# All steps of a planned kernel in a new order: both scaled copies of px ahead of both VectorE mixes

## The chip, the cores and the metric

The kernel runs on one core of a Trainium2 chip. The metric is the device time of one execution in microseconds (us). Engines are called TensorE (PE; its weight loads PEld), VectorE (DVE), ScalarE (ACT), GpSimd (POOL) and SyncE (SP), the last of which only issues DMAs here.

## The reference

Two layers follow one another, for a batch of 4 with 12288 positions of 128 channels each. The first is attention over 768 pooled keys, which are also the values:

```
kv_flat = kv.reshape(B, H//4, 4, W//4, 4, C).mean(axis=(2, 4)).reshape(B, -1, C) @ w_sr
s = (q @ kv_flat.transpose(0, 2, 1)) / sqrt(C)
a = exp(s - s.max(-1)); a /= a.sum(-1) + 1e-9
x = a @ kv_flat
```

The second mixes each position with the one before it and gates a squared ReLU:

```
xk = mu_k * x + (1 - mu_k) * x_prev
xr = mu_r * x + (1 - mu_r) * x_prev
v = maximum(xk @ w_k, 0) ** 2 @ w_v        # w_k 128 x 1024, w_v 1024 x 128
out = v / (1 + exp(-(xr @ w_r)))
```

## The kernel before, in words

The positions of all batches are cut into 96 tiles of 512 (24 to a batch). Each tile is a list of named steps, `plan_tile` (line 506); a step is a few instructions of one engine. For tile i, with s from 0 to 3 (quarters of 128 positions), f from 0 to 3 (quarters of the 1024 inner channels) and j from 0 to 5 (blocks of 128 keys):

- `qf` loads q (SP), `qh` and `ql` split it into two parts (ScalarE, GpSimd). `S`s is six products (three splits times two pieces of the keys) into a PSUM buffer S, `nm`s its negated row maximum (VectorE), `ex`s the exponential with its row sum (ScalarE), `rc`1 and `rc`3 the reciprocals of two sums (VectorE, two small instructions). `f1`s and `f2`s make the two half-precision parts of the scaled row, tile pp (ScalarE, VectorE); `tt`s transposes it by DMA into pT (SP).
- `AV`j is three products each, 18 in all, that sum up in one PSUM bank, px. From px ScalarE makes two scaled copies, `xek` and `xer`, one column to the right, and VectorE two mixes, `xk` and `xr`, which add px, scaled again, to the copy. `xck` and `xcr` (GpSimd) bring the last column of the tile before. `xkh`, `xrh` (VectorE) and `xkl`, `xrl` (GpSimd) split the mixes into two half-precision parts.
- `ha`f and `hb`f are four and two products into a PSUM buffer ph, `r`f the ReLU (ScalarE, tile rr), `k2`f the square (VectorE, but ScalarE for f = 2), `kh`f and `kl`f its two parts (`kl`0 to `kl`2 are GpSimd's; `kl`3 and `kh`2 VectorE's). `va`f and `vb`f are four and two products into the PSUM bank pv.
- `z` is three products into pz, `th` and `E` two functions of it (ScalarE), `T1`, `E1`, `g` and `o` (VectorE) the gate and its product with pv; `so` stores o (SP).

PSUM holds three buffers of two banks, which S and ph take in turn (eight in a tile), one bank for px and pz (and for the small products of the keys), and one for pv. Where two engines read one PSUM buffer, the second waits until the first is done, whichever the order written; so `xek` behind `xr` waits for it, and `z` waits until all four readers of px are done.

The first batch's keys and the split weights come from steps that occur once: `L_` loads into six buffers in turn, `pa` and `pb` products with w_sr, `ab` sums on VectorE, and steps beginning with w for the weights. The next batch's keys are made beside the tiles (`later_keys`, line 382, and `batch_prep`, line 424): twelve sums `br` on VectorE, one a tile, and then, in about four tiles, `pk`, `pt` (TensorE), `ks`, `v1` (ScalarE), `am`, `ex`, `ksv`, `dg`, `v2`, `xt`, `sv`, `uz`, `ksh` (VectorE), `ksl` (GpSimd). `pk` and `pt` take the bank of px, so that a `z` or a first `AV` behind them waits until `ks` or `v1` and `v2` have read it; `v20` reads the first `pt`, `v21` the second.

The order is written out in tables of due times. `plan.add(places[name] + base, name, fn, ...)` puts each step of each tile on one list, sorted by due time, and the instructions are issued in that order; each engine keeps it:

```python
if i < len(EARLY):
    places, base = EARLY[i], 0.0
elif i >= NTILES - len(LATE):
    places, base = LATE[i - (NTILES - len(LATE))], i * PERIOD
else:
    places, base = WHEN, i * PERIOD
```

`WHEN` holds for tiles 6 to 91, shifted by PERIOD = 19.3 from tile to tile, `EARLY` and `LATE` for the first six and last four tiles, `PREP` for a next batch's keys (from 18 periods after the batch's first tile) and `ONCE` for the rest. A due time only sorts: an instruction starts when its engine has come to it and its waits are over. All tiles in the steady state thus show the same order, in which steps of five or six tiles interleave.

Every instruction goes through one helper, so the profile puts all of them on line 37 and tells them apart by tile names.

Of the kernel before, what the change touches and what calls it, by code (L numbers as in the profile page):

```python
# [71 lines left out]
def tile_kernel(ctx, tc, qT, kv0, kvw, w_sr, mu_k, mu_r, w_k, w_v, w_r, outT):  # L72
# [730 lines left out]
    for i, (b, t) in enumerate(seq):  # L803
# [39 lines left out]
    "ksl": 94.358,  # L843
# [38 lines left out]
        "xek": 93.799, "xer": 93.801, "xr": 94.755, "xk": 94.904, "xkh": 96.037, "xrh": 96.843,  # L882
# [7 lines left out]
    },  # L890
    {
# [15 lines left out]
    },  # L907
    {
# [195 lines left out]
```

## Time and profile before

| what | value |
|---|---|
| median of 3 runs | 1945.48 us (1943.72 to 1945.65) |
| the profiled execution | 1945.21 us, span of its instructions 1943.4 us |
| mean granted clock of TensorE | 0.992 |
| busy: PE, DVE, ACT, POOL | 1883.7, 1801.5, 1693.8, 1096.1 us (97%, 93%, 87%, 56% of the span) |
| matmuls, other instructions of DVE, ACT, POOL | 8883; 2582, 2432, 784 |
| first S product of tile 0 | 26.63 us |

Busy is the time that an engine had an instruction under way, also one that is held up inside. Matmuls overlap one another, so a mean duration of 380 ns for a product does not mean that two take 760 ns. Some matmul records are missing from the trace, mainly of `vb`.

### The profile page before, as it was taken

Reading aid. Unit: us, or ns where it says so; the run is one execution under the profiler, and the core shown is the slowest. Engines: PE = TensorE matmul, PEld = TensorE weight load, DVE = VectorE, ACT = ScalarE, POOL = GpSimd, SP = SyncE. Lnnn points to the kernel's source line nnn. Section 1 sums busy time; section 2 is a strip of 40 time slices with the busy share of each in tenths; the row PEclk is TensorE's granted clock in tenths of the full one; section 3 lists DMA queues with packets and bytes.
Section 4 is the critical chain, followed back from the end, with each engine's and each line's share of the span. In section 5 each row is a group of like instructions: output and inputs, shape, how many; then the busy total and the mean of one; then the engine's idle time right before and its main releaser. Section 6 shows DMA issues by size and latency. Waiting matters only on the chain. (4 is left out here: it accounts for less than half of the span.)

```text
span 1943.4 us, 26996 instructions
## 1 busy us (share of the span) xinstructions
PE 1883.7 (97%) x8883; PEld 1042.4 (54%) x9022; DVE 1801.5 (93%) x2582; ACT 1693.8 (87%) x2432; POOL 1096.1 (56%) x784
## 2 busy tenths in 40 slices
PE   6699999999999999999999999999999999999999
PEld 4345555555555555555555555555555555555554
DVE  6899999999999999999999999999999999999998
ACT  3688989888989898988999898987899999999997
POOL 0365565565656565546565656565565555556565
PEclk9799999999999999999999999999999999999999
DMA  6546575545565656445465656554555554645452
GB/s 210 116 106 152 116 156 111 102 103 107 110 131 130 147 125 147 104 101 111 99 124 118 154 125 147 125 114 87 109 109 114 103 121 97 128 98 122 88 120 60
DMA packets 640524, 230.59 MB, mean 119 GB/s; under 512 B 606336, under 2 KB 608640, under 8 KB 640384
## 3 DMA queue, kind: packets, MB, share of 16 engines
q1 hardware_dynamic: 640384, 228.85, 54.5%
q8 instruction: 72, 1.18, 0.3%
q14 instruction: 68, 0.56, 0.1%
HBM read 52.63 MB, written 25.17 MB: 40 GB/s over the span
## 5 line engine op out<-in xcount | busy, mean ns | idle before, releaser
L37 POOL TENSOR_TENSOR kl<-kk,kh 128x1024 bf16<-128x1024 f32 x288 | 673.0, 2338 | 633.5 <-DVE kk L37 508.8
L37 DVE TENSOR_REDUCE nm<-S 128x1 f32<-128x768 f32 x384 | 364.8, 951 | 82.4 <-PE S L37 80.3
L37 PE MATMUL px<-pT,v 128*128 128x512 f16 x1728 | 420.7, 380 | 2.5 <-DVE xk L37 2.0
L37 ACT ACTIVATE rr<-ph 128x1024 f32<-128x1024 f32 x384 | 392.5, 1023 | 9.4 <-PE ph L37 8.1
L37 PE MATMUL S<-ksh,ql 128*128 128x512 f32 (+1 forms) x768 | 314.2, 409 | 13.9 <-ACT pe L37 4.8
L37 ACT ACTIVATE kh<-rr 128x1024 f16<-128x1024 f32 x288 | 306.1, 1063 | 1.7 <-PE pv L37 0.7
L37 PE MATMUL ph<-xkh,wkl 128*128 128x512 f16 x768 | 292.1, 380 | 15.9 <-ACT rr L37 15.4
L37 PE MATMUL pv<-kh,wvl 128*128 128x512 f16 x768 | 292.1, 380 | 2.8
L37 DVE SCALAR_TENSOR_TENSOR pp<-pe,rc,pp 128x768 f16<-128x768 f32 x288 | 291.6, 1037 | 1.0 <-ACT pp L37 0.5
L37 PE MATMUL ph<-xkh,wkh 128*128 128x512 f16 x768 | 291.9, 380 | 0.0
L37 PE MATMUL pv<-kh,wvh 128*128 128x512 f16 x768 | 291.1, 379 | 0.0
L37 PEld LDWEIGHTS <-v 128*128 128x128 f16 x1728 | 169.2, 98 | 207.1 <-issue 4.8
L37 ACT ACTIVATE pp<-pe,rc 128x768 f16<-128x768 f32 x288 | 259.3, 930 | 7.8 <-DVE rc L37 6.7
L37 ACT ACTIVATE pe<-S,nm 128x768 f32<-128x768 f32 x288 | 260.8, 906 | 5.1 <-DVE nm L37 4.9
L37 PE MATMUL S<-ksl,qh 128*128 128x512 f32 (+1 forms) x768 | 260.7, 339 | 0.4 <-DVE ksl L37 0.4
L37 PE MATMUL S<-ksh,qh 128*128 128x512 f32 (+1 forms) x768 | 260.4, 339 | 0.0
L37 PEld LDWEIGHTS <-wkh 128*128 128x128 f16 x1536 | 150.5, 98 | 188.1 <-issue 18.4
L37 DVE TENSOR_TENSOR kk<-ph,rr 128x1024 f32<-128x1024 f32 x192 | 233.1, 1215 | 0.4 <-ACT rr L37 0.4
L37 PE MATMUL ph<-xkl,wkh 128*128 128x512 f16 x768 | 228.7, 380 | 0.1
L37 ACT ACTIVATE xek<-px,s 128x512 f32<-128x512 f32 x96 | 66.2, 690 | 161.7 <-DVE xr L37 160.5
L37 PE MATMUL pv<-kl,wvb 128*128 128x512 bf16 x629 | 192.1, 381 | 2.8 <-DVE o L37 0.3
L37 POOL TENSOR_TENSOR ql<-qf,qh 128x512 fp32r<-128x512 f32 x96 | 122.6, 1277 | 121.0 <-ACT qh L37 111.2
(120 smaller groups left out, 2947.2 us busy)
## 6 DMA issues: line engine op xcount, KB each, us to landing
qf<-qT SPq DMA_DIRECT2D x96, 256.0 KB, 3.6
outT<-o SPq DMA_DIRECT2D x96, 256.0 KB, 3.3
kvt<-kvw SPq DMA_DIRECT2D x36, 512.0 KB, 4.4
pT<-pp SPq DMA_TRANSPOSE x384, 3.8
kva<-kv SPq DMA_DIRECT2D x8, 512.0 KB, 6.9
kvb<-kv SPq DMA_DIRECT2D x4, 512.0 KB, 5.8
raw<-moe_w_k SPq DMA_DIRECT2D x2, 512.0 KB, 6.2
raw<-moe_w_v SPq DMA_DIRECT2D x2, 512.0 KB, 5.7
```

What stands on the lines that cost most here:

```text
L37: return self.tc.keep_in_program_order(op(*args, **kwargs))
```

## The change

Only the five tables of due times change; the steps, their instructions, their buffers and PERIOD stay. In `WHEN` the order around px was, on ScalarE, `xer`, `xek`, `r2`, and on VectorE `xr`, `nm0`, `xk`, `nm1`, with due times in the order `xer`, `xr`, `xek`, `xk`; it becomes `xer`, `xek`, `xk`, `xr`. S2 and S3 move next to one another. A tile's steps reach over more periods: from S0 to `o` they were due 74 apart and are due 73 apart, but `qf` to S0 grows from 26 to 43. The key steps of `PREP` and the steps of the opening and the end get new places as well; in `ONCE` the loads come in another order (a3, a0, b0, a2, b2, a1, a5, a4, a7, b1, a6, b3 in place of b0, a0, a4, a2, a1, a5, b2, a7, a6, a3, b1, b3).

```diff
--- before.py
+++ after.py
@@ -819,230 +819,229 @@
 BUFS = {'pe': 4, 'nm': 4, 'sm': 4, 'rc': 4, 'pp': 4, 'kk': 3, 'kh': 4, 'kl': 4, 'kv': 6, 'rr': 2, 'ks': 1, 'acc': 1, 'dg': 1}
 
 WHEN = {
-    "br": 4.834, "qf": 9.313, "qh": 18.248, "ql": 20.178, "S0": 35.177, "nm0": 35.808, "S1": 36.66,
-    "nm1": 38.437, "ex0": 39.041, "ex1": 39.928, "S2": 40.62, "nm2": 40.667, "rc1": 43.604,
-    "ex2": 44.284, "S3": 46.007, "f10": 47.022, "nm3": 47.544, "f11": 47.928, "ex3": 48.229,
-    "f20": 50.413, "f21": 50.646, "rc3": 50.878, "f13": 50.928, "f23": 52.158, "f12": 52.946,
-    "f22": 53.836, "tt0": 54.549, "tt1": 59.807, "xcr": 59.944, "tt3": 61.596, "tt2": 65.088,
-    "AV3": 66.101, "AV0": 68.19, "AV2": 68.522, "AV4": 69.769, "xck": 70.195, "AV5": 70.881,
-    "AV1": 70.932, "xer": 72.783, "xr": 73.264, "xek": 75.33, "xk": 76.867, "xrh": 77.253,
-    "xkh": 77.561, "xkl": 79.579, "xrl": 80.391, "ha0": 83.258, "hb0": 83.665, "ha1": 85.358,
-    "r0": 85.436, "hb1": 85.71, "kh0": 88.135, "r1": 89.288, "k20": 89.788, "ha2": 90.5,
-    "hb2": 91.005, "kh1": 91.223, "va0": 91.315, "k21": 92.334, "kl0": 92.659, "r2": 94.751,
-    "kl1": 95.281, "ha3": 95.77, "hb3": 96.009, "vb0": 96.321, "va1": 96.586, "k22": 96.797,
-    "kh2": 97.398, "r3": 97.509, "kh3": 97.838, "k23": 98.43, "vb1": 98.624, "kl3": 98.729,
-    "z": 99.402, "E": 100.599, "va2": 101.251, "th": 102.036, "T1": 102.529, "E1": 102.851,
-    "kl2": 103.089, "va3": 104.612, "vb2": 106.923, "vb3": 107.016, "g": 109.079, "o": 109.515,
-    "so": 146.481,
+    "br": 1.042, "qf": 12.651, "qh": 29.016, "ql": 46.752, "S0": 55.51, "S1": 56.462, "nm0": 59.244,
+    "nm1": 59.67, "ex0": 60.617, "ex1": 62.496, "rc1": 63.617, "f10": 63.761, "S2": 64.341,
+    "S3": 64.75, "nm2": 65.854, "nm3": 66.223, "f20": 66.23, "ex2": 66.504, "ex3": 66.617,
+    "rc3": 68.48, "f13": 69.684, "f23": 71.528, "f12": 73.263, "f22": 73.431, "f11": 75.412,
+    "f21": 75.732, "tt0": 78.044, "tt3": 79.342, "tt2": 83.686, "tt1": 85.302, "AV3": 87.247,
+    "xck": 88.989, "AV5": 89.687, "xcr": 89.964, "AV0": 90.572, "AV2": 90.897, "AV4": 91.705,
+    "AV1": 93.901, "xer": 97.231, "xek": 97.76, "xk": 99.283, "xr": 100.465, "xkh": 101.525,
+    "xkl": 104.705, "ha0": 105.25, "hb0": 105.46, "r0": 105.904, "xrh": 107.258, "xrl": 108.051,
+    "ha1": 108.337, "kh0": 108.374, "hb1": 108.543, "k20": 108.572, "kl0": 109.492, "r1": 110.99,
+    "k21": 111.257, "ha2": 111.388, "hb2": 112.236, "kh1": 114.2, "kl1": 115.987, "r2": 116.16,
+    "k22": 117.885, "va0": 117.903, "ha3": 118.453, "kh2": 120.127, "hb3": 120.787, "vb0": 120.797,
+    "r3": 121.11, "k23": 121.696, "va1": 121.697, "kh3": 121.959, "z": 123.005, "vb1": 123.254,
+    "va2": 123.68, "va3": 123.751, "kl3": 124.012, "th": 124.096, "E": 124.174, "T1": 124.773,
+    "E1": 125.385, "kl2": 125.795, "vb2": 125.85, "g": 127.005, "vb3": 127.511, "o": 128.12,
+    "so": 138.819,
 }
 
 PREP = {
-    "pk0": -0.275, "ks0": 1.085, "pk1": 1.205, "ks1": 2.337, "am": 3.06, "ex": 11.539,
-    "ksv": 21.809, "dg": 32.144, "pt0": 38.416, "v10": 39.481, "v20": 40.224, "pt1": 45.363,
-    "v11": 45.606, "ksh": 45.752, "xt": 45.879, "v21": 46.14, "sv": 51.47, "uz": 62.598,
-    "ksl": 94.358,
+    "pk1": 5.405, "ks1": 5.658, "pk0": 8.519, "ks0": 9.073, "am": 10.692, "ex": 21.057,
+    "ksv": 36.458, "dg": 42.797, "pt0": 43.839, "v10": 44.144, "v20": 45.289, "pt1": 47.07,
+    "v11": 47.193, "xt": 47.663, "v21": 48.117, "sv": 48.854, "uz": 55.901, "ksh": 62.535,
+    "ksl": 82.678,
 }
 
 ONCE = {
-    "L_b0": 0.2, "L_a0": 0.28, "L_a4": 7.245, "L_a2": 9.413, "pa0": 10.197, "pa4": 10.199,
-    "L_a1": 11.332, "L_a5": 12.301, "ab0": 13.925, "pa2": 14.799, "pa1": 15.369, "pb0": 15.433,
-    "pa5": 15.956, "L_mu": 16.195, "L_b2": 16.197, "L_a7": 16.199, "ab2": 16.203, "pa7": 16.494,
...
+    "L_a3": 2.792, "pa3": 10.963, "L_a0": 11.208, "L_b0": 12.209, "L_a2": 12.223, "L_b2": 12.34,
+    "L_a1": 12.625, "L_mu": 12.966, "L_a5": 13.901, "pa0": 20.32, "L_a4": 23.133, "ab2": 23.232,
+    "ab0": 24.363, "mix": 26.596, "pa2": 27.02, "pa1": 27.54, "pa5": 28.025, "pb2": 29.962,
...
 }
 
 EARLY = [
     {
-        "qf": 9.512, "qh": 10.135, "ql": 13.854, "S0": 34.927, "S1": 35.512, "S2": 36.64, "nm0": 36.943,
...
+        "qf": 8.073, "qh": 25.93, "ql": 38.206, "S0": 53.725, "S1": 54.754, "S2": 54.893, "nm0": 54.93,
...
     },
...
 ]
 
 LATE = [
...
 ]
```

## Rows read from the trace of the kernel before

**Rows 1.** Busy time by stretch; columns: engine busy (instructions), granted clock, DMA share, GB/s.
```profile
0.00:26.63 26.63, 18.12 (x40) 8.09 (x41) 8.88 (x15) 3.12 (x4) 3.19 (x8) 1.00 0.90 319
26.63:77.90 51.27, 32.29 (x122) 23.41 (x121) 47.17 (x101) 33.29 (x60) 10.57 (x10) 0.80 0.51 105
...
343.10:467.60 124.50, 119.07 (x565) 65.89 (x573) 118.61 (x169) 106.10 (x155) 70.82 (x50) 1.00 0.49 103
...
658.50:812.30 153.80, 153.17 (x734) 85.44 (x744) 145.71 (x209) 139.10 (x200) 91.42 (x65) 1.00 0.60 133
812.30:937.80 125.50, 120.07 (x562) 66.24 (x570) 118.13 (x169) 106.06 (x154) 70.16 (x50) 0.99 0.48 101
...
1129.40:1283.30 153.90, 153.27 (x735) 85.41 (x745) 145.75 (x209) 139.15 (x200) 91.53 (x65) 1.00 0.60 132
1283.30:1408.90 125.60, 120.11 (x564) 66.22 (x571) 118.26 (x169) 106.07 (x154) 70.26 (x50) 0.99 0.50 101
...
1600.20:1753.20 153.00, 152.37 (x735) 84.85 (x745) 142.66 (x201) 139.90 (x200) 89.47 (x65) 1.00 0.53 111
...
1886.90:1943.40 56.50, 52.44 (x244) 25.32 (x246) 46.38 (x60) 43.11 (x55) 35.75 (x22) 1.00 0.33 76
```
**Rows 2.** The same view for instructions on px alone: PE, DVE, ACT busy.
```profile
812.30:937.80 125.50, 26.25 (x108) 8.86 (x13) 8.30 (x12) 0.99 0.48 101
...
1600.20:1753.20 153.00, 35.00 (x144) 11.87 (x17) 11.03 (x16) 1.00 0.53 111
```
**Rows 3.** Waits of the whole span: us in total, times, longest.
```profile
ACT xek L37 <- DVE xr L37: 160.5, 88, 4.3
...
DVE nm L37 <- PE S L37: 80.3, 96, 1.1
```
**Rows 4.** Waits from 812.3 to 937.8 us.
```profile
ACT xek L37 <- DVE xr L37: 16.4, 6, 4.3
...
PE ph L37 <- ACT rr L37: 4.8, 4, 1.8
```
**Rows 5.** Timeline of VectorE in a steady tile: start, duration, [idle before <-releaser].
```profile
1608.59 1.03 DVE L37 TENSOR_SCALAR rc<-sm 128x2 f32<-128x2 f32 x1
...
1620.75 0.96 DVE L37 TENSOR_REDUCE nm<-S 128x1 f32<-128x768 f32 x1 [1.08 <-PE S L37]
```
**Rows 6.** Timeline of GpSimd, at a boundary and in a steady tile.
```profile
849.23 2.13 POOL L37 TENSOR_TENSOR kl<-kk,kh 128x1024 bf16<-128x1024 f32 x1 [5.85 <-DVE kk L37]
...
1607.46 2.13 POOL L37 TENSOR_TENSOR kl<-kk,kh 128x1024 bf16<-128x1024 f32 x1
```
**Rows 7.** Timeline of VectorE at the second boundary.
```profile
848.98 2.47 DVE L37 TENSOR_SCALAR dg<-ident,ex,mtop 128x128 f32<-128x128 f32 x2
```
**Rows 8.** Timeline of ScalarE there.
```profile
855.72 0.69 ACT L37 ACTIVATE xek<-px,s 128x512 f32<-128x512 f32 x1 [4.29 <-DVE xr L37]
```
**Rows 9.** Timeline of TensorE there.
```profile
857.37 0.43 PE L37 MATMUL ph<-xkh,wkl 128*128 128x512 f16 x1 [1.83 <-ACT rr L37]
```
**Rows 10.** Instructions on one tile: duration in ns, min/median/max, first and last start.
```profile
L37 DVE TENSOR_SCALAR dg<-ident,ex,mtop x8: 336/340/2214, 36.4 to 1320.2; 128x128 f32<-128x128 f32 x8
...
L37 DVE TENSOR_SCALAR s<-mix,sv x8: 216/226/1982, 64.2 to 1346.5; 128x2 f32<-128x2 f32 x8
...
L37 DVE TENSOR_SCALAR rc<-sm x192: 149/160/1205, 33.4 to 1899.9; 128x2 f32<-128x2 f32 x192
```
**Rows 11.** TensorE's groups from 812.3 to 937.8 us: busy, mean ns | idle before.
```profile
L37 PE MATMUL pk<-acc,wsr 128*128 128x512 f32 (+1 forms) x4 | 1.7, 512 | 0.0
L37 PE MATMUL pt<-ident,ksv 128*128 128x128 f32 x6 | 1.4, 372 | 0.0
L37 PE MATMUL pt<-dg,ones 128*128 128x256 f32 x2 | 0.6, 380 | 0.0
```
**Rows 12.** The page's groups of instructions, whole span: busy, mean ns | idle before.
```profile
L37 ACT ACTIVATE rr<-ph 128x1024 f32<-128x1024 f32 x384 | 392.5, 1023 | 9.4 <-PE ph L37 8.1
...
L37 DVE TENSOR_TENSOR kk<-ph,rr 128x1024 f32<-128x1024 f32 x192 | 233.1, 1215 | 0.4 <-ACT rr L37 0.4
```

More of the change, by code (lines that the diff above doesn't have):

```diff
@@ L875 @@
     {
[6 rows of a table removed]
-        "xek": 93.799, "xer": 93.801, "xr": 94.755, "xk": 94.904, "xkh": 96.037, "xrh": 96.843,
[7 rows of a table removed]
-    },
-    {
[15 rows of a table removed]
-    },
-    {
[6 rows of a table removed]
-        "xcr": 112.942, "xek": 113.859, "xk": 114.929, "xer": 116.264, "xkh": 117.281, "xr": 120.059,
[8 rows of a table removed]
-    },
-    {
[6 rows of a table removed]
-        "xer": 134.366, "xr": 136.568, "xek": 136.908, "xck": 137.769, "xk": 139.491, "xkh": 140.916,
[8 rows of a table removed]
-    },
-    {
[6 rows of a table removed]
-        "xck": 149.549, "xek": 150.668, "xer": 150.675, "xr": 152.184, "xk": 153.263, "xkh": 155.63,
[8 rows of a table removed]
-    },
-    {
[15 rows of a table removed]
[14 rows of a table added]
+    },
+    {
[6 rows of a table added]
+        "xcr": 114.619, "xer": 114.923, "xek": 115.094, "xk": 115.68, "xr": 115.682, "xkh": 124.739,
[8 rows of a table added]
+    },
+    {
[6 rows of a table added]
+        "xek": 138.465, "xer": 139.8, "xcr": 141.0, "xk": 142.863, "xr": 142.981, "xkh": 145.851,
[8 rows of a table added]
+    },
+    {
[15 rows of a table added]
+    },
+    {
[15 rows of a table added]
+    },
+    {
[15 rows of a table added]
     },
@@ L979 @@
     {
[15 rows of a table removed]
-    },
-    {
[15 rows of a table removed]
-    },
-    {
[6 rows of a table removed]
-        "xck": 76.323, "xek": 77.9, "xer": 77.902, "xr": 78.688, "xk": 80.767, "xkh": 81.128,
[8 rows of a table removed]
-    },
-    {
[6 rows of a table removed]
-        "xer": 70.118, "xcr": 71.29, "xr": 71.447, "xek": 71.592, "xk": 73.052, "xkh": 78.145,
[8 rows of a table removed]
[6 rows of a table added]
+        "xer": 95.023, "xek": 95.808, "xck": 98.351, "xk": 100.553, "xr": 102.179, "xkh": 106.445,
[8 rows of a table added]
+    },
+    {
[6 rows of a table added]
+        "xek": 103.615, "xcr": 108.403, "xr": 108.721, "xck": 108.729, "xk": 108.891, "xkh": 112.331,
[8 rows of a table added]
+    },
+    {
[15 rows of a table added]
+    },
+    {
[6 rows of a table added]
+        "xek": 112.816, "xcr": 114.725, "xk": 116.049, "xkh": 116.167, "xkl": 117.486, "ha0": 118.425,
[7 rows of a table added]
     },
```

328 rows, old and new, of tables (EARLY, LATE, ONCE) are left out of this document.

## The prediction

> **What bounds the kernel now.** I read the busy table by stages first. From tile 80 to tile 88 eight tiles take 153.0 us and TensorE is busy for 152.37 of them [rows 1]; the count of px products, 18 a tile, shows that the stretch holds eight tiles and the boundary stretch six [rows 2]. So a steady tile costs 153.0/8 = 19.125 us, all of it TensorE's, and no order of steps makes that shorter: the change alters no product. What an order can win stands where TensorE isn't full. The same table shows three such places [rows 1]: the opening up to the first S product (26.63 us) and the stretch behind it (TensorE 32.29 of 51.27, VectorE 47.17), the three stretches in which the next batch's keys are made ready (six tiles in 124.5, 125.5 and 125.6 us), and the end (52.44 of 56.5).
>
> Then the waits. ScalarE's longest wait is for `xek` behind VectorE's `xr`, 160.5 us in 88 cases; VectorE's is `nm` behind TensorE, 80.3 us in 96 [rows 3]. The first looks like the prize of this change, but in the steady stretch it costs nothing, since TensorE has no gap there. VectorE's wait says how much room VectorE has: in the timeline `nm0` waits 1.08 us [rows 5]. There is room that can't be seen as idle time, too: `rc1` lasts 1.03 us [rows 5] where its median is 0.160 [rows 10], and it ends as GpSimd's `kl2` ends, 1607.46 + 2.13 [rows 6]. So 0.87 us of a tile is VectorE held up behind GpSimd.
>
> In the boundary stretch the wait for `xek` does reach TensorE. The chain, read at 849 to 857 us: `dg`, two small products due between `k20` and `o`, takes 2.47 us [rows 7], because GpSimd began `kl0` at 849.23 for 2.13 us [rows 6]; a `dg` product alone takes 0.340, and 2.214 at worst [rows 10]. All of VectorE's queue behind it moves, `xr` among it; `xek` waits 4.29 us [rows 8]; `r2` stands behind `xek` on ScalarE; and `ha3`, which needs the PSUM buffer that `r2` frees, stops TensorE for 1.83 us [rows 9]. In that stretch such waits for `rr` sum to 4.8 us [rows 4].
>
> **The change part by part.** It is an order only: same instructions, same sizes. In the steady table TensorE now runs S0 S1 va0 ha3 hb3 vb0 va1 S2 S3 z vb1 va2 va3 ha0 hb0 AV3 vb2 vb3 ha1 hb1, four AV, ha2 hb2 AV1.
>
> *The two copies first.* ScalarE's order is now kh1 r2 xer xek k22; VectorE's nm0 nm1 xk xr. `xek` no longer stands behind a VectorE step, so `r2`, and with it `ha3`, no longer inherit VectorE's lateness; `r2` even precedes both copies. In its place VectorE's first mix now waits for the second copy (`xk` reads `xek`), where `xr` needed the first alone. Queued behind `xk` on VectorE are `xr`, `kh2`, `xkh`, `rc1`; the first on TensorE to miss them is `z` (it needs the px bank) and then `ha0`. But `nm0` and `nm1` stand before `xk` and wait for S0 and S1, so that the copies are done by then: cost 0, at most VectorE's room, 1.08. Where that is gone, the cost shows as a wait of `z` or `ha0`.
>
> *Steady tiles.* `rc1` now stands right behind `xkh`, and GpSimd's next work, `xkl`, waits for that same `xkh`; so the 0.87 us of hold-up should go, and VectorE's room grows towards 1.08 + 0.87 = 1.95. The tiles stay at 19.125. The stretches with the key sums ran 0.8 and 0.9 us over 153.0 [rows 1], the tiles in which VectorE has one more reduction than its room holds; with the new room they fall back: -1.7, with 0 as the other end. The transposes of the pp tiles and the q loads keep their places behind what they wait for in SP's queue; the last transpose follows `f21` instead of `f22`, and AV3 is still more than half a tile away. Cost 0; a late one would show as a wait of AV3.
>
> *Boundaries.* Six steady tiles are 6 x 19.125 = 114.75, so the three lose 9.75 + 10.75 + 10.85 = 31.35 us. TensorE's own work for the keys is 1.7 + 1.4 + 0.6 = 3.7 each [rows 11], 11.1 in all; that stays. 20.25 us are waits, and that is the most that an order wins. Of these, 3 x 4.8 = 14.4 are the waits for `rr` just followed (I take the middle boundary for all three). They go for two reasons: the copies no longer tie ScalarE to VectorE, and the key steps leave the places where GpSimd is at work: `dg` now stands between `xr` and `kh2`, with GpSimd waiting for `xkh`; `sv` (its multiply 0.226 in the median, 1.982 at worst, [rows 10]) between `E1` and `rc3` instead of behind `k20`. `dg` and one `sv` multiply then give VectorE back some (2.214 - 0.340) + (1.982 - 0.226) = 3.6 us a batch, an estimate. Of the other 20.25 - 14.4 = 5.85 I take half, 2.9. Against this stand new waits: in one tile period come `dg`, both copies out of `pt`, `xt`, `sv` and `uz`; `pt0` holds the px bank until `v20` is through VectorE, `z` waits for it, and `v11` stands before `ex2` on ScalarE until the second `pt` is done. No row shows this order; per boundary it is between 0 and the longest TensorE wait there, 1.83. I take 0.8, 2.4 in all. Sum: -14.4 - 2.9 + 2.4 = -14.9, ends -20.25 and 0.
>
> *Opening.* Loads, key products and weight steps are all reordered. From 26.63 to 77.90 VectorE was busy for 92% of the time, so what counts is how much VectorE work precedes the first `xk` and `xr`: by the new list it is what it was, but for one key sum more and `f21` of tile 2 in place of `f22`. The load queue holds six key loads in flight in both orders; the later ones wait for a buffer, and one of these is now freed by `ab0`, which stands behind `ab2`. TensorE's work ahead of S0 of tile 8 is the same in both lists. I take 0, from -3 (part of VectorE's 4.1 idle us) to +19 (below).
>
> *End.* TensorE is 52.44 busy of 56.5, and what is left is the last `o` and its store: nothing to win but 0.5, and with `xr` of the last tile no longer between its copies the chain is shorter. I take +0.5 for a new gap, ends -0.5 and +3.
>
> **Sum.** The profiled execution took 1945.2 us, span 1943.4, 0.3 under the median of the runs. -14.9 - 1.7 + 0 + 0.5 = -16.1: 1929.
>
> **A rule against it.** That `dg` waits for `kl0` and `rc1` for `kl2` is in rows 5 to 7. The Trainium skill (SBUF — State Buffer, Who interferes with whom) says that VectorE and GpSimd share a port pair as a lock held for a whole instruction, and that a VectorE operation with two SBUF inputs takes part in it as well as the fast copies do. Here that would catch `f22`, which in the new order follows `k21`, close to `kl0`; by the rule alone the sum would move towards the second rival, by the rows it stays, since they show no `f2` held up in steady tiles.
>
> **Rivals.**
> 1. *The boundary's waits only change their place.* VectorE's key work is now packed into one tile, and TensorE stops at `z`, AV3 and `ha2` as long as it did at `ha3`. For it: VectorE is the engine with least room. Against: `dg` and `sv` alone get shorter. Then only -1.7 + 0.5 are left: 1944.
> 2. *Slower: `f22` behind `kl0` in each tile.* `kh0` frees `kl0` on GpSimd; `f22` follows it after `r1` and `k21`, 1.02 + 1.21 by [rows 12], against `kl0`'s 2.13. That is a tie, so the hold-up is near 0; if `kl0` begins later it is up to 2.13, and with `rc1` caught as before 3.0. It decides from 1.95 us a tile, VectorE's room: at 3.0 it costs 1.05 a tile, some 91 us over 87 tiles; half of that, less the 16, gives 1975.
> 3. *The opening is as late as its due times.* The first S of tile 0 was due at 34.9 and started at 26.63; the new list has it due at 53.7. If the loads truly come that much later, 18.8 us are added: 1948. Against: due times only sort the steps, and VectorE's work before the first mix is not more.
>
> **How the numbers follow.** Forecast 0.60 (1929, own range 1921 to 1938), rival 1 0.18, rival 2 0.07, rival 3 0.15. A measurement of this kernel tells 0.2%, 3.9 us, from no change. Faster by more takes the forecast's 0.60 nearly whole (0.59) and parts of rivals 1 and 3 (0.05 and 0.04): 0.68; within: 0.01 + 0.11 + 0.05 = 0.17; slower: 0.02 + 0.07 + 0.06 = 0.15. Low end: -20.25 - 1.7 - 3 - 0.5 = -25.5, 1919.7, set to 1919. High end: rivals 1 and most of 3 are taken in, 1947; what is above, mainly rival 2, and the little below are under 2 in 10.
>
> **What would show it.** Right: the wait of `xek` for `xr` is gone; eight tiles in 153.0; `rc1` near 0.160; six-tile stretches of the keys at 119 to 121 with few waits for `rr`; `dg` products near 0.340. Wrong: boundaries still at 124 or more with waits of `pz`, px or S in place of ph (rival 1); eight tiles above 154 with `pp` of over 1.2 us on VectorE (rival 2); the first S product, or tile 8's, more than 10 us later (rival 3).

## The result, and the profile after

The changed kernel takes 1920.55 us, the median of 4 runs (1919.19 to 1921.45), against 1944.6 of the kernel before beside it (1939.58 to 1945.65): ratio 0.9881, interval 0.9862 to 0.99. Repeated with the experiments it took 1919.66 (0.9875, 0.9859 to 0.989). The profiled execution took 1919.19, so against the 1945.2 of before the working of the forecast is missing 26.0 - 16.1 = 9.9 us. The starts of S0 of tile 8 and of the last tile, read from TensorE's timeline in both traces, split it:

| part | before | after | change | forecast |
|---|---|---|---|---|
| up to S0 of tile 8 | 187.9 | 185.8 | -2.1 | 0 |
| boundaries: what their tiles take over 19.125 each | 30.8 | 11.1 | -19.7 | -14.9 |
| the other tiles up to the last | 1668.1 | 1664.4 | -3.7 | -1.7 |
| from S0 of the last tile to the end | 56.6 | 56.1 | -0.5 | +0.5 |
| span | 1943.4 | 1917.4 | -26.0 | -16.1 |

The 30.8 stands against 31.35 in the prediction, because the first stretch of [rows 1] ends inside the next tile. The S0 of tile 22 begins 0.6 us ahead of 467.60, on TensorE's timeline before:

```profile
466.99 0.58 PE L37 MATMUL S<-ksh,ql 128*128 128x512 f32 x1
```

First the page's busy times after: TensorE nearly as before (1883.7), VectorE 47 us less for the same 2582 instructions. Busy includes time in which an instruction is held up. The groups that shrank most are `rc` (67.3 to 32.3 us for 192) and `xrh` (59.0 to 39.5 for 96), so this is mostly hold-up that went.

```profile
span 1917.4 us, 26966 instructions
...
PE 1881.0 (98%) x9022; PEld 1033.4 (54%) x9022; DVE 1754.2 (91%) x2582; ACT 1699.9 (89%) x2432; POOL 1069.0 (56%) x784
```

The busy table by stretch, columns as in [rows 1]; the stretches begin at the S0 of tiles 24, 32, 40, 64, 80 and the last:

```profile
495.40:648.60 153.20, 153.20 (x747) 84.56 (x745) 144.16 (x207) 140.19 (x201) 87.48 (x65) 1.00 0.61 135
648.60:803.00 154.40, 154.40 (x749) 85.03 (x748) 144.92 (x208) 140.91 (x203) 87.55 (x65) 1.00 0.60 126
803.00:920.30 117.30, 116.38 (x569) 64.28 (x567) 109.32 (x168) 105.90 (x153) 68.18 (x50) 1.00 0.54 108
1265.70:1382.80 117.10, 116.16 (x568) 64.12 (x567) 109.23 (x168) 105.85 (x153) 68.10 (x50) 1.00 0.54 109
1574.20:1727.30 153.10, 153.10 (x745) 84.44 (x744) 137.84 (x201) 140.09 (x201) 87.57 (x65) 1.00 0.55 111
1861.30:1917.40 56.10, 52.52 (x248) 25.52 (x246) 45.75 (x60) 43.63 (x55) 36.11 (x22) 1.00 0.32 71
```

Eight steady tiles take 153.1, against 153.0 before. The six tiles that took 125.5 in [rows 1] take 117.3, but the key products `pk` now fall into the last tile of the stretch ahead (20.45; so its 154.4): 1.32 there and 2.37 in the one long tile behind it (21.50), 3.7 a boundary where it was 10.3.

The longest waits of the whole span (us in total, times, longest):

```profile
POOL xrl L37 <- DVE xrh L37: 326.6, 92, 5.7
POOL kl L37 <- ACT kh L37: 226.2, 175, 6.7
POOL xkl L37 <- DVE rc L37: 180.9, 85, 3.7
ACT th L37 <- PE pz L37: 59.4, 78, 1.3
DVE nm L37 <- PE S L37: 59.3, 60, 2.5
```

ScalarE's wait of `xek` for `xr`, first in [rows 3], is gone. The one wait of TensorE left in the second boundary, from the table of waits of 803.0 to 920.3, is a new one:

```profile
PE pt L37 <- DVE xr L37: 0.9, 1, 0.9
```

Its cause is in the timelines of VectorE, GpSimd and TensorE at that place (start, duration, [idle before <-releaser]):

```profile
820.68 1.01 DVE L37 SCALAR_TENSOR_TENSOR pp<-pe,rc,pp 128x768 f16<-128x768 f32 x1
821.61 0.62 DVE L37 TENSOR_SCALAR ksv<-ks,ivs 128x768 f32<-128x768 f32 x1
822.13 2.93 DVE L37 SCALAR_TENSOR_TENSOR pp<-pe,rc,pp 128x768 f16<-128x768 f32 x1
824.99 1.81 DVE L37 TENSOR_REDUCE nm<-S 128x1 f32<-128x768 f32 x2
826.72 0.74 DVE L37 SCALAR_TENSOR_TENSOR xk<-px,s,xek 128x512 f32<-128x512 f32 x1
827.38 0.73 DVE L37 SCALAR_TENSOR_TENSOR xr<-px,s,xer 128x512 f32<-128x512 f32 x1
828.04 0.59 DVE L37 TENSOR_SCALAR dg<-ident,ex,mtop 128x128 f32<-128x128 f32 x2
...
822.10 2.15 POOL L37 TENSOR_TENSOR kl<-kk,kh 128x1024 bf16<-128x1024 f32 x1 [1.36 <-ACT kh L37]
...
828.17 0.66 PE L37 MATMUL pt<-ident,ksv 128*128 128x128 f32 x4 [0.92 <-DVE xr L37]
```

The two `dg` take 0.59 together, where they took 2.47 in [rows 7]. But `ksv`, which the new order puts here, pushes `f21` just behind the start of `kl1` (822.10), and `f21` lasts 2.93 instead of 1.01: 0.03 us of lateness cost 1.9. Both mixes, and with them `pt0`, come late by that. This is the rule that the prediction set against itself: the Trainium skill (SBUF — State Buffer, Who interferes with whom) lets a two-input VectorE operation wait for GpSimd's whole instruction, and the trace agrees, though in one tile of each boundary and not in every tile as rival 2 had it. In a steady tile `rc1`, 1.03 in [rows 5], is no longer held; VectorE's timeline after:

```profile
1605.12 0.17 DVE L37 TENSOR_SCALAR rc<-sm 128x2 f32<-128x2 f32 x1
```

### The profile page after: what moved, and what is told of

Read it like the earlier page. It is cut to its first block, busy times and chain, and to the rows that moved or that the text cites. A ratio compares the mean times of both kernels' runs of the same rounds, so it can differ in the third digit from the quotient of the medians.

```text
span 1917.4 us, 26966 instructions
## 1 busy us (share of the span) xinstructions
PE 1881.0 (98%) x9022; PEld 1033.4 (54%) x9022; DVE 1754.2 (91%) x2582; ACT 1699.9 (89%) x2432; POOL 1069.0 (56%) x784
## 4 chain that ended last, share of the span: by engine, by line
PE 94%; DVE 3%; ACT 1%; DMA 1%; issue 1%; SPq 0%; DVEq 0%
PE pv L37 26%; PE ph L37 25%; PE S L37 20%; PE px L37 19%; PE pz L37 3%; DVE pp L37 1%; DVE nm L37 1%; PE pk L37 0%; DMA kva<-kv 0%; DMA kvb<-kv 0%; ACT pp L37 0%; PE pt L37 0%; DVE top L37 0%; ACT rr L37 0%; SPq L37 0%
## 5 line engine op out<-in xcount | busy, mean ns | idle before, releaser
L37 POOL TENSOR_TENSOR kl<-kk,kh 128x1024 bf16<-128x1024 f32 x288 | 653.8, 2271 | 240.5 <-ACT kh L37 226.2
L37 POOL TENSOR_TENSOR xrl<-xr,xrh 128x512 f16<-128x512 f32 x96 | 146.3, 1524 | 326.6 <-DVE xrh L37 326.6
L37 PE MATMUL S<-ksh,ql 128*128 128x512 f32 (+1 forms) x768 | 299.0, 389 | 8.9 <-ACT pe L37 4.7
L37 POOL TENSOR_TENSOR xkl<-xk,xkh 128x512 f16<-128x512 f32 x96 | 113.7, 1184 | 198.8 <-DVE rc L37 180.9
L37 PE MATMUL pv<-kl,wvb 128*128 128x512 bf16 x768 | 213.2, 379 | 0.0
```

Of the source, the lines that this page charges most:

```text
L37: return self.tc.keep_in_program_order(op(*args, **kwargs))
```

## The experiments

Three theories. **A**: what costs is a tie: `r2` stands on ScalarE behind a copy (`xek`), that copy behind a VectorE step (`xr`), and `ha3` on TensorE needs `r2`. **B**: what costs are the key steps (`dg`, `sv`) where GpSimd runs a `kl`, which hold VectorE up. **C**: it is the rest of the new order. Where a diff below is on the kernel before it is named so; the others are on the changed kernel. "Excess" is what a boundary's tiles take over the steady tile; by the starts of S0 it was 9.2, 10.8 and 10.8 in the kernel before, 10.3 in the mean, and it is 3.7 in the changed one.

**e1: the kernel before, with both copies ahead of both mixes, and no other step moved.**

```diff
-"xer": 72.783, "xr": 73.264, "xek": 75.33, "xk": 76.867
+"xer": 72.783, "xr": 73.264, "xek": 72.9, "xk": 73.2
```

> The order of before with one VectorE step moved in the steady table: xk stands ahead of xr and nm0, so that both copies of px precede both mixes; all other orders are those of before. Theory A (the copy xek behind VectorE's mix ties ScalarE's r2 to VectorE, and that is how the late VectorE of a key boundary stops TensorE): the waits of ph for rr, 4.8 us a boundary, go, and the time falls by 10 to 15 us, to 1930-1935. Theory B (VectorE is late because its key steps stand where GpSimd is at work, and the order of the copies is beside the point): 1942-1946. Theory C (the steady room of VectorE and the whole new order are needed): 1936-1944.

Measured 1925.27 (1922.7 to 1926.64), ratio 0.9903, 0.9887 to 0.992. The waits of `ph` for `rr` are gone, the excess falls to 4.4. Two due times bring 18.5 of the 24 us, more than any of the three theories said.

**e2: the changed kernel with `xr` between the two copies.**

```diff
-"xr": 100.465
+"xr": 97.4
```

> The order of after with xr put back between the copies in the steady table (xer, xr, xek, xk, with xr ahead of nm0 on VectorE); all else as after. Theory A: where VectorE is late at a boundary, xek and with it k22, ex0 and r3 are late too, some waits of TensorE return, 1922-1932. Theory B: no change, 1919-1922. Theory C: 1920-1925.

Measured 1923.14 (1921.6 to 1924.19), ratio 0.9896, 0.9881 to 0.9911. `xek` waits for `xr` again, 79.5 us in 85 cases, and it costs at most 3.5 us: the tiles show 1.9 in the two behind the opening, 0.4 at each boundary and nothing in a steady tile. So it isn't this wait that costs; A holds only if something that TensorE needs stands behind it, and here `r2` precedes both copies.

**e3: the changed kernel with the key steps put back.**

```diff
-"dg": 42.797, ... "sv": 48.854
+"dg": 31.5, ... "sv": 50.8
```

> The order of after with only dg and sv of the later batches' keys put back to where they stood before, between k20 and o, where kl0 begins on GpSimd. Theory A: VectorE loses some 3.6 us a batch but TensorE doesn't see it, 1919-1923; dg and sv products of over 1.9 us are seen. Theory B: the boundaries lose again, 3 x 2 to 3 x 5 us, 1926-1935. Theory C: 1921-1926.

Measured 1924.01 (1921.35 to 1925.55), ratio 0.99, 0.9885 to 0.9915: 4 us slower than the changed kernel, which only C's range holds. But not as B has it. In the view of the tile `dg` (ns: least, median, most) none is held up; in this order those places don't meet a `kl`:

```profile
L37 DVE TENSOR_SCALAR dg<-ident,ex,mtop x8: 337/340/342, 52.2 to 1285.9; 128x128 f32<-128x128 f32 x8
```

The multiplies of `sv` aren't held up either (229 ns at most), so e3 doesn't test B; e4 does, in the old order. The boundaries lose 0.85, 2.0 and 0.85 us against the changed kernel. At the second, `uz`, which was not moved, now begins just behind a `kl` and takes 2.11 where it took 0.22; the timelines of VectorE and GpSimd:

```profile
847.70 2.11 DVE L37 TENSOR_SCALAR uz<-cz,xt 128x3 f32<-128x3 f32 x1
...
847.64 2.15 POOL L37 TENSOR_TENSOR kl<-kk,kh 128x1024 bf16<-128x1024 f32 x1 [1.37 <-ACT kh L37]
```

Of the 0.85, 0.2 stands as a longer wait of `pt` for `xr` and 0.2 as a wait of `ph` for `kl3`; the rest isn't shown.

**e4: the kernel before with the key steps moved instead.**

```diff
-"dg": 32.144, ... "sv": 51.47
+"dg": 31.7, ... "sv": 51.0
```

> The order of before with only dg and sv moved a little ahead, between rc3 and g, where GpSimd is idle. Theory A: less lateness comes to xr, so part of the waits for rr goes, 1934-1940. Theory B: most of them go, 1928-1936. Theory C: 1940-1945.

Measured 1930.43 (1927.65 to 1931.92), ratio 0.9933, 0.9918 to 0.9947. Here `dg` is no longer held up (342 ns at most, 2214 in [rows 10]) and the waits for `rr` of the three boundaries are down from 14.4 to 7.0, with the tie still there. In the table of waits of the whole span:

```profile
PE ph L37 <- ACT rr L37: 7.8, 14, 0.9
...
ACT xek L37 <- DVE xr L37: 150.2, 88, 2.8
```

The excess is 5.6. Eight tiles with key sums still take 153.9.

**e5: the kernel before with the edits of e1 and e4 together.**

> The order of before with both edits that were tried alone: xk ahead of xr and nm0 (1925.3 alone), dg and sv ahead of g (1930.4 alone). Theory A (ScalarE is tied to VectorE by xek) and theory B (VectorE is late by key steps at GpSimd) together: the edits attack the same waits, so they don't add up; what the boundary still lost in the first (4.4 us each against 3.7 of key products) shrinks a little: 1921-1925, as the changed kernel or up to 3 us behind. Theory C (the rest of the new order has a part of its own): 3 us or more behind the changed kernel.

Measured 1919.13 (1915.6 to 1919.41), ratio 0.9867, 0.9853 to 0.9881: the changed kernel's time, with four due times instead of five tables, and 2 us under what A and B said. The excess is 2.45, in two tiles of 20.46 and 20.25, with no wait of TensorE in the boundary. e1 gave 18.5 and e4 13.3, both together 25.1: each takes away part of the same loss. C isn't needed for the gain.

**e6: the changed kernel with `pt0` later, behind the four products of a `va`.**

```diff
-"pt0": 43.839, "v10": 44.144
+"pt0": 44.55, "v10": 44.6
```

> The order of after with the first pt of the later batches' keys behind va1 instead of ahead of it: its wait for xr, 0.92 us at each of three boundaries, is filled by va1. Theory A and C: 0 to 2.8 us under the changed kernel, 1917-1920. Rival: v10, v20 and z are later by the same amount and the wait moves to z, no change.

Measured 1920.86 (1920.51 to 1923.47), ratio 0.9883, 0.9869 to 0.9897: no gain. `pt0` doesn't wait now, `z` does, which needs the bank that `v20` on the late VectorE has to read; TensorE's timeline:

```profile
833.12 0.38 PE L37 MATMUL pz<-xrh,wrl 128*128 128x512 f16 x1 [1.18 <-DVE v L37]
```

**e7: the kernel before with `r2` ahead of `xek` on ScalarE; VectorE's order untouched.**

```diff
-"xek": 75.33
+"xek": 75.5
```

> The order of before with one ScalarE step moved: r2 ahead of xek in the steady table; VectorE, TensorE, GpSimd and the queue as before, xek still behind xr. Theory A, in its narrow form (it is r2 behind xek that stops ha3): the waits of ph for rr go, 1928-1935. Rival D (what the copies-first edit gave is VectorE's: xk fills its idle time ahead of nm0): VectorE is as late as before and TensorE stops somewhere else, 1939-1945.

Measured 1927.22 (1922.47 to 1927.88), ratio 0.991, 0.9896 to 0.9924. One swap on ScalarE, no VectorE step earlier, and 17 us are gone: A in its narrow form. Eight tiles with key sums in the busy table:

```profile
649.00:802.00 153.00, 152.37 (x733) 84.88 (x744) 143.83 (x208) 140.87 (x201) 89.66 (x65) 1.00 0.60 133
```

The stretch that took 153.8 [rows 1] takes 153.0 here too.

The path shows itself in the last tile of the second boundary, where both kernels have the same hold-up: an `f2` behind GpSimd's `ksl`, 2.32 instead of 1.01. VectorE before, VectorE in e7, and the wait of TensorE that only the kernel before has behind it:

```profile
916.39 2.32 DVE L37 SCALAR_TENSOR_TENSOR pp<-pe,rc,pp 128x768 f16<-128x768 f32 x1
...
901.56 2.32 DVE L37 SCALAR_TENSOR_TENSOR pp<-pe,rc,pp 128x768 f16<-128x768 f32 x1
...
921.05 0.38 PE L37 MATMUL ph<-xkh,wkl 128*128 128x512 f16 x1 [0.92 <-ACT rr L37]
```

That tile takes 20.20 before and 19.15 in e7. The same lateness of VectorE costs 1.05 us with the tie and nothing without it.

**e9 and e12: the tie put back into the changed kernel, whole and half.** e9 has `xr` between the copies and `r2` behind both; e12 has only `r2` behind both.

```diff
 e9
-"xr": 100.465, ... "r2": 116.16
+"xr": 97.4, ... "r2": 117.1
 e12
-"r2": 116.16
+"r2": 117.1
```

> The changed kernel with two steps put back: xr between the copies (xer, xr, xek, xk) and r2 behind both copies on ScalarE, so that ha3 again hangs on VectorE's xr through xek and r2. Theory A (this tie is what carries VectorE's lateness to TensorE): waits of TensorE for rr come back, 1 to 2 us in one or two tiles of a boundary, 3 to 6 us a boundary in all or 5 to 15 us over the three; time 1926 to 1935. Theory C (the tie matters only beside key steps that stand where GpSimd works, and these stay moved here): waits for rr below 1 us a boundary, time 1920 to 1925, as with xr alone between the copies (1923.1).

> The changed kernel with ScalarE's order alone altered: r2 behind both copies (kh1 xer xek r2) instead of ahead of them; xr stays behind both copies on VectorE. It is the fourth corner beside the changed kernel (1919.7), xr alone between the copies (1923.1) and both (1964.8, 19.58 a steady tile). Tie theory (r2 costs only where xek ahead of it waits for a VectorE step): 1918 to 1925, steady tiles 19.10 to 19.16, no wait of xek. Rival (r2 is late behind two copies of 0.69 each and the wait for px, whatever VectorE does): waits of ph for rr of 0.2 to 0.5 in each tile, tiles of 19.3 to 19.6, 1935 to 1965.

e9 takes 1964.78 (1963.93 to 1965.38), ratio 1.0108, 1.0093 to 1.0123: slower than the kernel before, outside what either theory said. e12 takes 1918.86 (1917.17 to 1921.09), ratio 0.9874, 0.9857 to 0.989: nothing. With e2 and the changed kernel these are the four corners: `r2` late costs nothing, `xr` between the copies 3.5, both together 45. Eight tiles of e9 in the busy table and in its waits:

```profile
507.70:664.40 156.70, 154.43 (x747) 83.97 (x745) 148.65 (x207) 141.15 (x200) 88.39 (x64) 1.00 0.57 131
```

```profile
ACT xek L37 <- DVE xr L37: 7.1, 8, 0.9
...
DVE xr L37 <- ACT xer L37: 3.9, 8, 0.8
ACT xer L37 <- PE px L37: 3.4, 8, 0.6
...
PE ph L37 <- ACT rr L37: 2.3, 8, 0.3
```

A tile takes 156.7/8 = 19.59, 0.46 more than 19.125, some 40 us over 87 tiles. The waits show a chain across three engines in each tile, px to `xer` to `xr` to `xek` to `r2` to `ha3`. The kernel before had the same chain and lost nothing in steady tiles: there TensorE had 22 products between the last of px and `ha3` (`ha` and `hb` of another quarter, `va`, S0, S1), in the new order the 16 of S0, S1 and `va0`. 2.3 of the 3.7 us of eight tiles stand as waits for `rr`; where the other 1.4 lie these views don't show.

**e10: e9 with the key steps put back as in e3.**

> The same two steps put back, and the key products dg and the sv multiplies put back to the places in the tile that they had before (behind k20, where GpSimd runs kl0). Everything else keeps the new order. Theory A with B (tie and key steps together are the whole gain): the boundaries lose some 8 to 10 us each again and the time goes to 1935 to 1944. Theory C (the rest of the new order carries a share by itself, in the boundary's neighbours and the tiles with key sums): 1922 to 1930, with boundary waits for rr of at most 3 us each.

Measured 1983.59 (1978.75 to 1984.76), ratio 1.0207, 1.019 to 1.0224, again outside both. Without the tie these key steps cost 4 us (e3), with it 19. How lateness travels, from the timelines of VectorE, GpSimd, ScalarE and TensorE at the second boundary:

```profile
845.58 2.91 DVE L37 SCALAR_TENSOR_TENSOR pp<-pe,rc,pp 128x768 f16<-128x768 f32 x1
848.41 0.74 DVE L37 SCALAR_TENSOR_TENSOR xr<-px,s,xer 128x512 f32<-128x512 f32 x1
...
845.04 2.63 POOL L37 TENSOR_TENSOR kl<-kk,kh 128x1024 bf16<-128x1024 f32 x1 [1.37 <-ACT kh L37]
...
849.18 0.69 ACT L37 ACTIVATE xek<-px,s 128x512 f32<-128x512 f32 x1 [2.97 <-DVE xr L37]
849.77 1.01 ACT L37 ACTIVATE rr<-ph 128x1024 f32<-128x1024 f32 x1
...
850.84 0.38 PE L37 MATMUL ph<-xkh,wkl 128*128 128x512 f16 x1 [2.37 <-ACT rr L37]
```

None of the moved key steps is held up here either (`dg` 341 ns at most); they push other steps behind a `kl`. `kl1` holds `f21`, `f21` makes `xr` late, `xr` holds `xek`, `r2` stands behind it, and `ha3` stops TensorE for 2.37. In the changed kernel the same `f21` of 2.93 costs TensorE 0.92, at `pt0`. At the other two boundaries of e10 it is `ksv` that is held, 2.53 instead of 0.61.

**e11: the changed kernel with `ksv` alone moved, between `f20` and the next tile's `T1`.**

```diff
-"ksv": 36.458
+"ksv": 28.0
```

> The changed kernel with ksv alone moved: from between f22 and f21 to between f20 and the first multiply of the next px, so that f21 isn't pushed behind kl1 on GpSimd (2.93 us at 822.13 in the changed kernel, 0.9 us of wait of pt0 for xr behind it). Theory (f21 held up by kl1 makes VectorE late, and pt0 pays): f21 near 1.2 in the boundary tile, the wait of pt for xr gone in all three boundaries, 0.9 to 1.1 us each, time 1916.5 to 1918. Rival (VectorE is late in this tile by the sum of its key steps, wherever ksv stands): the wait moves to z or ha0 at the same size, 1919 to 1921.

Measured 1916.83 (1915.11 to 1917.67), ratio 0.986, 0.9846 to 0.9875. VectorE's and GpSimd's timelines at the same place, and the busy table of the six tiles:

```profile
818.82 1.94 DVE L37 SCALAR_TENSOR_TENSOR pp<-pe,rc,pp 128x768 f16<-128x768 f32 x2
821.77 2.01 DVE L37 TENSOR_REDUCE nm<-S 128x1 f32<-128x768 f32 x2 [1.02 <-PE S L37]
...
820.24 2.54 POOL L37 TENSOR_TENSOR kl<-kk,kh 128x1024 bf16<-128x1024 f32 x1 [1.36 <-ACT kh L37]
```

```profile
801.20:918.40 117.20, 117.20 (x574) 65.21 (x573) 107.77 (x168) 106.83 (x154) 68.87 (x50) 1.00 0.56 111
```

`f22` and `f21` now take 1.94 together, VectorE even waits for S0 again (1.02), and TensorE has no wait in the boundary. The long tile falls from 21.47 to 21.50 to 20.33 to 20.36 in all three boundaries, 3.4 us in all. The intervals of the two kernels overlap, as they weren't timed side by side; it is the three tiles that show the gain. Of all kernels run this has the lowest time.

## Why the prediction was right, and where it was not

The forecast of 1929 was 8 us too slow; 1920.55 lies at the low end of the range, just below the forecast's own 1921 to 1938. Of the missing 9.9 us 4.8 are the boundaries', 2.1 the opening's, 2.0 the other tiles' and 1.0 the end's.

**Steady tiles and what bounds them**: right, 153.0 before and 153.1 after. Most of the time was to be won at the boundaries, and there 19.7 of the 26.0 us were won.

**The step that was mis-sized** is the sum of the boundaries: -14.4 for the waits for `rr`, -2.9 for half of the rest, +2.4 for new waits. Two of its parts were off.

- What goes. All that the old order lost there went, not half of the rest. e7 and e1 show why: with the tie alone cut the excess falls by 5 to 6 a boundary, with the key steps alone by about 5 (e4), with both to 2.45 (e5). The waits of `ph` for `rr` were that part of the lateness which stood in the table; each effect covered part of the other, and adding waits of one name under-counted it.
- What stays. The 3.7 of the keys' own products came from busy times of products that overlap. The tiles of e5 and e11 without any wait show 2.45 and 2.5. So at least 30.8 - 3 x 2.45 = 23.4 was to be won, not 20.25 at most; the change took 19.7 of it, and e11 most of the rest.

The new waits, +2.4, were near in size (3 x 0.92 = 2.8 as waits, 3.4 by the tiles of e11) and in the steps named (`pt0`, the px bank). The price was guessed between bounds, so that is luck in part: the prediction had `z` waiting for `pt0`'s bank, but it is `pt0` that waits for the late `xr`, and the cause, `f21` behind `kl1`, was not foreseen.

**The two copies first**: the reason was right and is now narrower. Not the order of copies and mixes as such, but that no step which TensorE needs stands on ScalarE behind a step that waits for VectorE: e7 reaches it with the mixes unmoved, e12 keeps it with `r2` moved back, and e9 loses 45 us.

**Steady -1.7**: measured -3.7. The tiles with key sums and their neighbours gave -2.0, near the forecast, but by luck, for the cause was wrong. The prediction took the hold-up of `rc1` from a stretch without key sums [rows 5]; in the stretch that it priced, `rc1` was hardly ever held. The view of the tile `rc` before, from 658.5 to 812.3 and from 1600.2 to 1753.2 us:

```profile
L37 DVE TENSOR_SCALAR rc<-sm x16: 157/159/896, 668.4 to 806.4; 128x2 f32<-128x2 f32 x16
...
L37 DVE TENSOR_SCALAR rc<-sm x16: 158/596/1041, 1608.6 to 1747.2; 128x2 f32<-128x2 f32 x16
```

One of the 16 in the first is above 0.2 us, eight in the second, where the tiles took their 19.125 all the same. With the tie cut by the one swap of e7 the stretch takes 153.0, and e4, without that cut, keeps 153.9: those tiles were late by the tie. (`xrh`, 0.68 at most there before, is 0.42 in e7; whether the cut works in part through it isn't separated.) Another -2.2 came in the eight tiles behind the opening, which the prediction had not priced; e7 has about half of that too. The tiles from 70 on cost 0.5 more, which no run explains.

**Opening**: 0 holds. The -2.1 is within what one order gives from run to run: S0 of tile 8 begins at 183.8 to 188.4 us in nine executions with the new opening, at 183.7 to 189.1 in five with the old one. Rival 3 is refuted: the first S begins at 26.2, though it was due at 53.7. **End**: -0.5, the low end of its range.

**Rival 1** (waits only change place) is what e6 shows for one wait, but not for the boundary. **Rival 2** (`f22` behind `kl0` in each tile) didn't come in steady tiles; its mechanism came with `f21` and `kl1`, three times. The kernel before had it three times too, with `ksl` (2.32, under e7).

## What to carry to other kernels

Look for chains that cross engines twice in one tile: a step that the bounding engine needs, queued behind a step that waits for another engine. A wait that costs nothing in steady tiles (160.5 us of waits in all here) is the path on which any lateness of the other engine travels, and cutting it can be one swap on the engine in between. Before adding up waits by name, subtract what the same stretch takes when nothing waits, measured on a tile, not from durations that overlap.

## What the runs showed of the hardware

- A VectorE operation with two SBUF inputs that begins 0.03 us behind a GpSimd `kl` takes 2.93 us instead of 1.01. With the order of the two turned (e11, the pair of `f2` from 818.82 to 820.76, `kl` from 820.24) it is the `kl` that is longer, 2.54 in place of 2.14 to 2.15. The Trainium skill (SBUF — State Buffer, Who interferes with whom) says that issue order decides who blocks; these rows agree.
- A held-up operation counts as busy: a `dg` held behind `kl0` stands with 2.214 us where 0.340 is the median, and VectorE's busy time fell by 47 us with the same instructions.
